# Attention and two gated layers on one core: a pair's reciprocals made one step earlier and sent ahead of the half's bulk loads, and the raw keys' load moved behind them

## The chip, the cores and the metric

The kernel runs on 1 core of one Trainium2 chip. The metric is the device time of one execution in microseconds (us). Before the change the median of 3 runs is 1176.01 us (1171.54 to 1176.41).

## The reference, cut to what matters

```python
def _attn_ref(q, k, v):                      # 4 x 8 heads, 1152 positions, 64 wide
    q_pool = q.reshape(B, H, S // 2, 2, D).mean(axis=3)
    scores = scale * np.matmul(q_pool, k.transpose(0, 1, 3, 2))
    scores = scores - np.max(scores, axis=-1, keepdims=True)
    attn = np.exp(scores)
    attn = attn / (np.sum(attn, axis=-1, keepdims=True) + 1e-09)
    return np.matmul(attn, v)

x = attn_out.transpose(0, 2, 1, 3).reshape(2304, 512)
h = x @ moe_w_in;  x = (h - np.tanh(h)) @ moe_w_out                 # 512 -> 2048 -> 512
h = x @ moe2_w_in; x = (h / (1.0 + np.exp(-1.702 * h))) @ moe2_w_out
```

Each attention row is divided by its sum of exponentials at the end. The change touches only when the reciprocals of these sums are made and sent, and when the keys of a later pair are loaded.

## The kernel before, in words

Two heads make a pair, and there are 16 pairs. The 576 pooled queries of a pair are worked on in two halves of 288, so there are 32 halves: half h belongs to pair h // 2, and an even half is a pair's first one. All 32 halves stand in one loop (L668), with one order of instructions per engine and no scheduler: what is written first is issued first. The attention takes about the first 390 us; the two gated layers behind it are not touched.

In a half, the tensor engine (PE) makes nine score tiles `sc` (`scores`, L414: keys and queries are each split into a rounded high part, `kh`, `qh`, and a rest, `kl`, `ql`; the fourth product, `sel` with `row`, subtracts the row maxima), the scalar engine (ACT) exponentiates them to `pf`, and PE multiplies these with the values (`products`, L473, tile `acc`). Between the score tiles PE makes products `mx` for the row maxima of the next pair (`unit`, L344), which the vector engine (DVE) reduces (L371). The PSUM pool has four buffers, taken in turn by `sc`, `mx` and `acc`.

- The maxima go from columns to a row by DMA: `send_rows` (L380) transposes them (`tt`) and issues small DMAs from SP's queue to `row` and `cr`. Six of them are issued late in an odd half (L388); the first score tile of the next even half needs them.
- The sums of a finished pair go the other way: `sums` (L509) sends them into columns at the start of the next pair's even half (tile `s`), `recip` (L519) adds two parts and takes reciprocals on DVE (L522, L523) and writes them to memory (`rd`, L525), `spread` (L528) reads them back spread over 64 partitions (`rbd`, two DMAs, L531) at the start of the odd half, and `normalise` multiplies with them at that half's end.
- The loads: `load_k` (L287) brings the raw keys `kr` of a pair two ahead (576 KB, two buffers), `load_v` (L292) the values of the next pair (576 KB), `load_sum` (L284) the summed queries `qs` of the pair two ahead (288 KB), `fetch_low` (L339) the queries' low parts `ql` (288 KB). SP issues all of these. GpSimd (POOL) issues two adding DMAs a pair (L281, L338).
- In the next odd half ACT rounds the queries and then the raw keys (`prep_qh`, L306; `prep_kh`, L321); POOL makes the low parts of the keys (`prep_kl`, L328), one part at the end of an even half, one at the end of an odd half. On POOL `kl` waits, by a dependence added by hand, for the job that stands in `last["v"]` (L330): in an even half that is the pair's reciprocal.
- On DVE stand also `rest` additions (L464), `end_rows` (L392) and steps that convert weights (`wt`, L143 to L163), one step a half.

Named places in a half set the order: `first` and `start` ahead of the score tiles, `load`, `pre` and `gp` behind them, then `products`, then `end` and `pool`.

Of the kernel before, what the change touches and what calls it, by code (L numbers as in the profile page):

```python
# [23 lines left out]
def f32(ap):  # L24
    return ap.bitcast(F32)
# [3 lines left out]
def tile_pooled_attention_two_moe(  # L29
# [189 lines left out]
    def attention(ctx: ExitStack):  # L219
# [19 lines left out]
        rows = [ap.tile([128, SP], F32R, name=f"row{i}") for i in range(2)]  # L239
# [133 lines left out]
        def max_rows(p, part, out=None):  # L373
            d = pairs[p]
            mt = f32(d["mt"][:, 0:30]).rearrange("p (c j) -> p j c", c=3)
            at, n = (0, 6) if part == 0 else (6, 4)
            out = d["m3"][:, at:at + n] if out is None else out
            nc.vector.tensor_reduce(out, mt[:, at:at + n, :], AX.X, ALU.min)

        def send_rows(p, part):  # L380
            d = pairs[p]
            tt = ap.tile([128, 32], F32R, tag="tt", name="tt", bufs=2)
            nc.vector.transpose(f32(tt[:]), f32(d["m3"][:]))
            for c in range(6 * part, 6 + 4 * part):
                j, s = divmod(c, 2)
                row = f32((d["row"] if j < 4 else d["cr"])[:])
                q0 = 128 * j if j < 4 else 0
                nc.sync.dma_start(  # L388
                    out=row[64 * s:64 * s + 1, q0:q0 + 128].rearrange("o (a i) -> o a i", i=32),
                    in_=f32(tt[c:c + 97:32, :]))  # L390

        def end_rows(p):  # L392
            d = pairs[p]
            nc.vector.tensor_reduce(
                d["row"][:, 512:], f32(d["cr"][:]).rearrange("p (h i) -> p i h", h=2),
                AX.X, ALU.min)
# [17 lines left out]
        def scores(g, some=slice(0, 4)):  # L414
            p, i = divmod(g, 2 * KT)
            x, t = divmod(i, KT)
            d = pairs[p]
            sc = opened.pop(g, None)
            if sc is None:
                sc = ps.tile([128, 2, 512], F32, tag="ps", name="sc")  # L420
            else:
                some = slice(3, 4)
            ks, xs = slice(128 * t, 128 * t + 128), slice(HB * x, HB * x + HB)
            steps = (
                (d["kh"][:, ks], d["qh"]), (d["kl"][:, ks], d["qh"]),
                (d["kh"][:, ks], d["ql"]), (sel, d["row"]))
            for n, (w, m) in list(enumerate(steps))[some]:
                for s, r in enumerate(sides):
                    nc.tensor.matmul(  # L429
                        sc[:, s, 0:HB], w[r], m[r, xs], start=(n == 0), stop=(n == 3))  # L430
            if some.stop < 4:
                opened[g] = sc
                return
            pf = ap.tile([128, 2, HB], F32, tag="pf", name="pf", bufs=10)
            nc.scalar.activation(pf, sc[:, :, 0:HB], AF.Exp, scale=SCALE)  # L435
            probs[g] = pf

        def add(p, x, t):
            new = probs[(2 * p + x) * KT + t]
            if t == 0:  # L440
                parts[p, x] = new
                return
            out = parts[p, x]
            if t == 1:
                out = ap.tile([128, 2, HB], F32, tag="sum", name="sum")
            job = nc.gpsimd.tensor_add(out, parts[p, x], new)  # L446
            parts[p, x] = out
            return job

        def full(p, x):  # L450
            return 1 < 2 * p + x < 2 * NPAIR - 1

        def rest_of(p, x):
            return ((5, 6, 7, 8),) if full(p, x) else ((5, 6), (7, 8))

        def add_rest(p, x, t):
            n, group = next((n, g) for n, g in enumerate(rest_of(p, x)) if t in g)
            new = probs[(2 * p + x) * KT + t]
            if t == group[1]:
                rests[p, x, n] = ap.tile([128, 2, HB], F32, tag=f"two{5 + 2 * n}", name="rest")  # L460
                prev = probs[(2 * p + x) * KT + group[0]]
            else:
                prev = rests[p, x, n]
            job = last["rest"] = nc.vector.tensor_add(rests[p, x, n], prev, new)  # L464
            if full(p, x) and t == group[1]:
                after(add(p, x, KADD - 1), job)

        def add_two(p, x, t):
            two = [probs[(2 * p + x) * KT + i] for i in (t - 1, t)]
            pairs[p]["twos"].append(ap.tile([128, 2, HB], F32, tag=f"two{t}", name="two"))  # L470
            nc.vector.tensor_add(pairs[p]["twos"][-1], *two)
# [74 lines left out]
        def at(h, when, fn, *args):  # L546
            jobs.setdefault((h, when), []).append(lambda: fn(*args))

        def do(h, when):
            for job in jobs.pop((h, when), ()):  # L550
                job()
# [3 lines left out]
        NH = 2 * NPAIR  # L555
# [32 lines left out]
        for p in range(NPAIR):  # L588
            h = 2 * p
            if p > 0:  # L590
                at(h - 2, "load", load_v, p)
                if p == 1:
                    at(h - 2, "pre", prep_corner, p)
                    at(h - 2, "end", prep_ql, p)
                    at(h - 2, "pool", prep_kl, p, 0)
                    at(h - 1, "end", prep_kl, p, 1, nc.vector)
                else:
                    at(h - 2, "pool", prep_kl, p, 0)
                    at(h - 1, "pool", prep_kl, p, 1)
                    at(h - 1, "first", fetch_low, p, "ql")  # L600
                at(h, "start", sums, p - 1)
                at(h, "pre" if h == NH - 2 else "end", recip, p - 1)
                at(h + 1, "start", spread, p - 1)
                at(h + 1, "end", normalise, p - 1)
            if p > 1:
                at(h - 4, "start", new_pair, p)
                at(max(h - 6, 0), "start", load_one, p)
                at(max(h - 6, 0), "gp" if p > 2 else "start", load_other, p)
                at(h - 4, "load", load_sum, p)
                at(h - 4, "first", load_k, p)  # L610
                at(h - 3, "pre", prep_qh, p)
                at(h - 3, "pre", prep_corner, p)
                at(h - 3, "pre", minus_qh, p)
                at(h - 3, "pre", prep_kh, p, 0)
                at(h - 3, "pre", prep_kh, p, 1)
                at(h - 3, "gp", take_qh, p)
# [13 lines left out]
        first, second = slice(0, 128), (slice(128, 2 * 128), slice(2 * 128, 3 * 128))  # L630
# [37 lines left out]
        for h in range(NH):  # L668
            p, x = divmod(h, 2)
            do(h, "first")  # L670
            do(h, "start")
            g = h * KT
            t = 0
            late = [t for g in rest_of(p, x) for t in g[1:]] if h < NH - 1 else []
            for u in todo[h]:
                if u is None:
                    scores(g + t)
                    if h < NH - 1 and t < KADD - full(p, x) or t < 4:
                        add(p, x, t)
                    elif h == NH - 1 and t in (5, 7):  # L680
                        add_two(p, x, t)
                    t += 1
                    if t == KT and late and h != 1:
                        add_rest(p, x, late.pop(0))
                    continue
                unit(*u)
                if u == (p + 1, 6):
                    max_rows(p + 1, 0)
                    send_rows(p + 1, 0)
                if u == (p, 10):  # L690
                    max_rows(p, 1)
                    send_rows(p, 1)
                if t == KT and late:
                    add_rest(p, x, late.pop(0))
                    if late and x == 0 and full(p, x):
                        add_rest(p, x, late.pop(0))
                        end_rows(p)
            while late:
                add_rest(p, x, late.pop(0))
            if h == NH - 2:  # L700
                end_rows(p)
            do(h, "load")
            do(h, "pre")
            do(h, "gp")
            products(p, x)
            if x == 0 and not full(p, x):
                end_rows(p)
            do(h, "end")
            do(h, "pool")
# [603 lines left out]
    with tc.manual_schedule():  # L1313
        with ExitStack() as c1:
            ending = attention(c1)
        with ExitStack() as c2:
            moe(c2, ending)
# [44 lines left out]
```

## Time and profile before

| | |
|---|---|
| median of 3 runs | 1176.01 us (1171.54 to 1176.41) |
| profiled execution, its own time | 1176.05 us |
| its span, first to last instruction | 1174.3 us |
| mean granted clock of TensorE | 0.998 |
| PE busy | 1161.6 us (99%) |
| DVE busy | 992.5 us (85%) |
| ACT busy | 652.9 us (56%) |
| POOL busy | 453.6 us (39%) |

The profiled execution took 1.75 us more than its span. Busy times are those of the whole span; in a chain of work, each step is named by what it waited for or by the instruction before it on its engine.

### The profile page before, as it was taken

How to read it: one execution, taken by the hardware profiler on the slowest of the kernel's cores; microseconds unless marked ns; L12 is line 12 of the kernel's file. 1: busy time of each engine (PE TensorE's matmuls, PEld its weight loads, DVE VectorE, ACT ScalarE, POOL GpSimd, SP SyncE). 2: the span in 40 equal slices, each digit the busy share in tenths (PEclk: the TensorE clock that was granted, in tenths of full speed). 3: DMA queues.
4: the chain of work that ended last, by engine and by line, in shares of the span. 5: the costliest groups of instructions: out<-in, count | busy, mean ns of one | idle time of the engine just before them, and what ended most of it. 6: DMA issues, size and time to landing. Idle time of an engine off the chain costs nothing.

```text
span 1174.3 us, 23203 instructions
## 1 busy us (share of the span) xinstructions
PE 1161.6 (99%) x9260; PEld 971.5 (83%) x9260; DVE 992.5 (85%) x1242; ACT 652.9 (56%) x969; POOL 453.6 (39%) x321
## 2 busy tenths in 40 slices
PE   9999999999999999999999999999999999999998
PEld 7767676767777888888898898898889999999996
DVE  6888988878988799999999999998986899886442
ACT  4667566656665678676666666655654333342220
POOL 7667676766766223333232333221000222222211
PEclk9999999999999999999999999999999999999999
DMA  6455655555542021111111111112998757765512
GB/s 191 123 118 137 162 127 133 146 143 130 125 111 62 12 64 36 55 54 37 54 36 54 37 36 36 37 54 95 389 389 311 275 215 287 269 225 206 206 54 90
DMA packets 58221, 156.29 MB, mean 133 GB/s; under 512 B 14080, under 2 KB 19712, under 8 KB 58112
## 3 DMA queue, kind: packets, MB, share of 16 engines
q1 hardware_dynamic: 53536, 146.14, 35.8%
q0 software_dynamic: 4032, 8.26, 4.9%
q8 instruction: 73, 1.20, 0.4%
q10 hardware_dynamic: 544, 0.39, 0.1%
q14 instruction: 36, 0.29, 0.1%
HBM read 124.39 MB, written 33.69 MB: 135 GB/s over the span
## 4 chain that ended last, share of the span: by engine, by line
PE 77%; DVE 14%; ACT 4%; issue 2%; DMA 1%; POOL 1%; SPq 1%; DVEq 0%; ACTq 0%; POOLq 0%
PE sc L429 13%; PE y L1048 13%; PE y L1236 12%; PE h L1139 11%; PE acc L480 11%; PE b L996 5%; PE a L996 3%; PE c L996 3%; PE mx L359 3%; DVE work L1182 2%; DVE work L1199 2%; DVE wt L149 2%; DVE wt L143 1%; ACT work L1180 1%; PE acc L493 1%
## 5 line engine op out<-in xcount | busy, mean ns | idle before, releaser
L371 DVE TENSOR_REDUCE mt<-mx 128x2 fp32r<-128x1024 f32 (+2 forms) x176 | 198.1, 1136 | 41.0 <-PE mx L359 22.1
L435 ACT ACTIVATE pf<-sc 128x576 f32<-128x576 f32 x288 | 173.8, 655 | 24.2 <-PE sc L429 15.1
L1236 PE MATMUL y<-mem,big 128*128 128x512 f32 (+1 forms) x780 | 185.1, 368 | 1.2 <-POOL mem L1153 1.2
L1236 PEld LDWEIGHTS y<-mem,big 128*128 128x128 f32 x780 | 142.6, 188 | 21.2 <-POOL mem L1153 2.3
L1034 POOL TENSOR_TENSOR mem<-work,mem 128x768 fp32r<-128x768 f32 x24 | 46.2, 1938 | 289.4 <-ACT mem L1029 274.4
L446 POOL TENSOR_TENSOR sum<-sum,pf 128x576 f32<-128x576 f32 x95 | 137.4, 1446 | 29.2 <-DVE rest L464 23.9
L480 PE MATMUL acc<-pf,v 128*32 128x288 f32 x2304 | 146.3, 407 | 0.0
L1139 PE MATMUL h<-mem,big 128*128 128x512 f32 (+1 forms) x564 | 127.1, 377 | 0.0
L480 PEld LDWEIGHTS acc<-pf,v 128*32 128x32 f32 x2304 | 71.6, 110 | 65.6 <-ACT pf L435 5.0
L1139 PEld LDWEIGHTS h<-mem,big 128*128 128x128 f32 x564 | 104.4, 188 | 17.0
L1153 POOL TENSOR_TENSOR mem<-work,mem 128x1024 fp32r<-128x1024 f32 (+1 forms) x40 | 89.1, 2227 | 75.9 <-ACT mem L1151 75.9
L1048 PE MATMUL y<-big,mem 128*128 128x512 f32 x405 | 114.0, 390 | 0.0
L1201 ACT ACTIVATE work<-work 128x1024 f32<-128x1024 f32 (+1 forms) x40 | 39.1, 977 | 107.5 <-DVE work L1199 107.5
L429 PE MATMUL sc<-qh,kh 64*128 64x288 f32 x576 | 94.0, 315 | 0.0
L171 POOL TENSOR_TENSOR big<-wt,big 128x512 fp32r<-128x512 f32 x25 | 32.6, 1302 | 155.5 <-ACT big L170 142.5
L429 PE MATMUL sc<-row,sel 64*128 64x288 f32 x576 | 88.5, 293 | 3.9 <-DMA row<-tt 2.4
L1048 PEld LDWEIGHTS y<-big,mem 128*128 128x128 f32 x405 | 76.0, 188 | 15.5
L429 PE MATMUL sc<-qh,kl 64*128 64x288 f32 x576 | 87.5, 293 | 0.0
L429 PE MATMUL sc<-ql,kh 64*128 64x288 f32 x576 | 87.2, 292 | 0.0
L1139 PE MATMUL h<-mem,w 128*128 128x512 f32 (+1 forms) x376 | 84.7, 377 | 0.0
L501 ACT ACTIVATE u<-acc 128x576 f32<-128x576 f32 x30 | 19.6, 653 | 107.3 <-PE acc L493 107.3
L1139 PEld LDWEIGHTS h<-mem,w 128*128 128x128 f32 x376 | 69.6, 188 | 11.3
(176 smaller groups left out, 2580.5 us busy)
## 6 DMA issues: line engine op xcount, KB each, us to landing
mem<-x SPq DMA_DIRECT2D x36, 768.0 KB
big<-x SPq DMA_DIRECT2D x27, 768.0 KB
raw<-in_moe_w_in_dram SPq DMA_DIRECT2D x32, 512.0 KB
raw<-in_moe_w_out_dram SPq DMA_DIRECT2D x32, 512.0 KB
v<-in_v_dram SPq DMA_DIRECT2D x16, 576.0 KB
x<-big SPq DMA_DIRECT2D x12, 768.0 KB
kr<-in_k_dram SPq DMA_DIRECT2D x15, 576.0 KB
rbd<-rd SPq DMA_DIRECT2D x32, 144.0 KB
```

Of the source, the lines that this page charges most:

```text
L371: nc.vector.tensor_reduce(out, src, AX.X, ALU.max, negate=True)
L429: nc.tensor.matmul(sc[:, s, 0:HB], w[r], m[r, xs], start=(n == 0), stop=(n == 3))
L435: nc.scalar.activation(pf, sc[:, :, 0:HB], AF.Exp, scale=SCALE)
L446: job = nc.gpsimd.tensor_add(out, parts[p, x], new)
L480: nc.tensor.matmul(acc[32 * n:32 * n + 32, 0], pairs[p]["v"][:, s, t, 32 * h:32 * h + 32], new[t][:, s, :], start=(t == 0), stop=(t == KT ...
L996: nc.tensor.matmul(bank[nm][:, fp, 0:G], w[:, wo, a, 128 * c:128 * c + 128], x[:, b, c, :], start=(k == 0), stop=(k == 5))
L1034: eng.tensor_tensor(g[:, :, 1], halves[n][:, fp], f32(g[:, :, 0]), op=ALU.subtract)
L1048: nc.tensor.matmul(y, gts[2 * side + fp][:, j, r, 128 * t:128 * t + 128], wo[:, p, :], start=(k == 0), stop=(k == len(terms) - 1))
L1139: nc.tensor.matmul(hb[:, j, 0:TBS[b]], wi[:, c, w, :], x[r][c], start=(k == 0), stop=(k == 3 * NKC - 1))
L1153: eng.tensor_tensor(gt[:, :, 1, :], g, f32(gt[:, :, 0, :]), op=ALU.subtract)
L1201: nc.scalar.activation(a, u, AF.Relu, bias=-T2)
L1236: nc.tensor.matmul(ys[m][:, 0:w], lhsT, rhs, start=(fp == 0 and not low and j == p == 0), stop=(fp == 1 and low and j == 1))
```

## The change

Three lines change. The reciprocals of pair p - 1 are made at a new place, `rows`, which is run right behind `end_rows` in an even half; before, they were made at the half's `end`, behind `products`. The load of the raw keys of pair p moves from the start of half 2p - 4 (`first`) to its `load` place, where it is the last in the list.

```diff
-                at(h, "pre" if h == NH - 2 else "end", recip, p - 1)
+                at(h, "pre" if h == NH - 2 else "rows", recip, p - 1)
...
                 at(h - 4, "load", load_sum, p)
-                at(h - 4, "first", load_k, p)
+                at(h - 4, "load", load_k, p)
...
                     if late and x == 0 and full(p, x):
                         add_rest(p, x, late.pop(0))
                         end_rows(p)
+                        do(h, "rows")
```

On SP's queue, from the even half of pair 2 to the rows that its odd half sends, the order before was this (`s` the sums, `qd` the queries in memory, `r` the reciprocals):

```order
L290 DMA kr<-in_k_dram 128x1152
L514 DMA s_101<-u 64x1x9 x4
L278 DMA qd<-in_q_dram 128x576
L388 DMA row_96<-tt 1x4x32 x2
L388 DMA cr_98<-tt 1x4x32 x2
L294 DMA v<-in_v_dram 128x1152
L285 DMA qs<-qd 128x576
L525 DMA rd<-r_1310 128x9
L342 DMA ql<-qd 128x576
L531 DMA rbd<-rd 64x576 x2
L388 DMA row_97<-tt 1x4x32 x6
```

And it is this now:

```order
L514 DMA s_101<-u 64x1x9 x4
L278 DMA qd<-in_q_dram 128x576
L388 DMA row_96<-tt 1x4x32 x2
L388 DMA cr_98<-tt 1x4x32 x2
L525 DMA rd<-r_1255 128x9
L294 DMA v<-in_v_dram 128x1152
L285 DMA qs<-qd 128x576
L290 DMA kr<-in_k_dram 128x1152
L342 DMA ql<-qd 128x576
L531 DMA rbd<-rd 64x576 x2
L388 DMA row_97<-tt 1x4x32 x6
```

`rd` has gone ahead of `v` and `qs`, and `kr` from the top to a place between `qs` and `ql`.

SP's DMAs use eight semaphores in turn (DMAHW0 to DMAHW7), and each waits on its own for the DMA that used it before. Now, from `kr` on, these waits are:

```order
L290 DMA kr<-in_k_dram 128x1152 [waits DMAHW2_49,Pool_49]
L342 DMA ql<-qd 128x576 [waits DMAHW3_49,DMASW4_49]
L531 DMA rbd<-rd 64x576 [waits DMAHW7_49,DMAHW4_49]
L531 DMA rbd<-rd 64x576 [waits DMAHW5_49]
L388 DMA row_97<-tt 1x4x32 [waits DMAHW6_49,DVE_49]
L388 DMA row_97<-tt 1x4x32
L388 DMA row_97<-tt 1x4x32 [waits DMAHW0_49]
L388 DMA row_97<-tt 1x4x32 [waits DMAHW1_49]
L388 DMA row_97<-tt 1x4x32 [waits DMAHW2_49]
L388 DMA row_97<-tt 1x4x32 [waits DMAHW3_49]
```

The fifth of the six row DMAs now waits for the landing of `kr` (DMAHW2), the sixth for that of `ql` (DMAHW3); before, these two waited for `rd` and `ql`.

On DVE, at the end of the same even half, this piece of the difference shows the move:

```order
 L464 TENSOR_TENSOR rest<-rest,pf 128x576 x2
 L394 TENSOR_REDUCE row_96<-cr_98 128x64
-L371 TENSOR_REDUCE mt_90<-mx 128x2
-L156 SCALAR_TENSOR_TENSOR wt<-wa,wt 128x512
-L522 TENSOR_REDUCE r_1310<-s_101 128x9
-L523 RECIPROCAL r_1310<-r_1310 128x9
+L522 TENSOR_REDUCE r_1255<-s_101 128x9
+L523 RECIPROCAL r_1255<-r_1255 128x9
+L371 TENSOR_REDUCE mt_90<-mx 128x2
+L156 SCALAR_TENSOR_TENSOR wt<-wa,wt 128x512
 L371 TENSOR_REDUCE mt_90<-mx 128x2 x2
```

The two instructions of the reciprocal now stand ahead of the half's last reduction of maxima and of the weights' step; in every second even half that step is L143 in place of L156.

## Rows read from the trace of the kernel before

**Rows 1.** The chain that ended last: start, length (us), what.

```profile
81.52 4.50 PE acc L480 x72
...
94.73 4.50 PE acc L480 x72
...
106.34 4.50 PE acc L480 x72
...
118.03 4.50 PE acc L480 x72
...
164.50 4.50 PE acc L480 x72
...
188.41 4.50 PE acc L480 x72
...
234.93 4.50 PE acc L480 x72
...
261.77 4.50 PE acc L480 x72
```

**Rows 2.** Stretch, length; busy PE, PEld, DVE, ACT, POOL; clock, DMA share, GB/s.

```profile
254.10:257.60 3.50, 3.50 (x32) 3.50 (x32) 1.90 (x4) 1.74 (x3) 1.02 (x1) 0.51 0.58 171
```

**Rows 3.** SP's queue in time, halves 6 and 7: start, length (us), DMA.

```profile
94.56 0.38 SPq L294 DMA_DIRECT2D v<-in_v_dram  x1
...
100.60 0.33 SPq L525 DMA_DIRECT2D rd<-r  x1
...
104.48 1.92 SPq L531 DMA_DIRECT2D rbd<-rd  x2
106.50 3.28 SPq L388 DMA_DIRECT2D row<-tt  x6
```

**Rows 4.** SP's queue in time, halves 18 and 19.

```profile
240.76 0.33 SPq L525 DMA_DIRECT2D rd<-r  x1
...
246.21 2.15 SPq L531 DMA_DIRECT2D rbd<-rd  x2
248.45 3.29 SPq L388 DMA_DIRECT2D row<-tt  x6
```

**Rows 5.** DVE in time: the transpose ahead of half 19's rows.

```profile
245.45 0.21 DVE L383 STREAM_TRANSPOSE tt<-m 128x32 f32<-128x32 f32 x1
```

**Rows 6.** DMA in two stretches of halves 6 and 18 (columns as in rows 2).

```profile
94.60:99.10 4.50, 4.50 (x78) 2.41 (x80) 4.40 (x6) 0.60 (x2) 2.12 (x3) 1.00 0.62 197
...
240.00:246.20 6.20, 6.20 (x88) 5.88 (x88) 5.07 (x10) 5.78 (x10) 5.96 (x6) 1.00 0.74 153
```

**Rows 7.** ACT in time, half 7: the keys' rounding and the next idle time.

```profile
108.14 1.24 ACT L321 ACTIVATE kh<-kr 128x576 fp32r<-128x576 f32 x2
111.40 0.66 ACT L501 ACTIVATE u<-acc 128x576 f32<-128x576 f32 x1 [2.02 <-PE acc L493]
```

**Rows 8.** DVE in time, the end of half 8.

```profile
121.76 0.28 DVE L394 TENSOR_REDUCE row<-cr 128x64 fp32r<-128x128 f32 x1
121.96 1.21 DVE L371 TENSOR_REDUCE mt<-mx 128x2 fp32r<-128x1024 f32 x1
123.09 0.68 DVE L156 SCALAR_TENSOR_TENSOR wt<-wa,wt 128x512 f32<-128x512 f32 x1
...
123.90 0.21 DVE L523 RECIPROCAL r<-r 128x9 f32<-128x9 f32 x1
124.03 1.22 DVE L371 TENSOR_REDUCE mt<-mx 128x2 fp32r<-128x1024 f32 x1
```

**Rows 9.** POOL in time: `kl` of half 8, and two sums of half 18.

```profile
124.20 1.43 POOL L328 TENSOR_TENSOR kl<-kr,kh 128x576 fp32r<-128x576 f32 x1 [3.07 <-DVE r L523]
...
232.10 2.93 POOL L446 TENSOR_TENSOR sum<-sum,pf 128x576 f32<-128x576 f32 x2
```

**Rows 10.** DVE in time: the same addition beside an idle and a busy POOL.

```profile
81.95 0.75 DVE L464 TENSOR_TENSOR rest<-pf 128x576 f32<-128x576 f32 x1
...
234.29 1.36 DVE L464 TENSOR_TENSOR rest<-pf 128x576 f32<-128x576 f32 x1
```

## The prediction

> **What bounds the kernel now.** I read the shares of busy time first, then the chain of work that ended last through the attention, and then the timelines of SP and DVE where that chain was interrupted. PE is busy 99% of the span, so only what PE loses can be won. The chain is a row of `acc` steps, and from one to the next a half can be timed: half 6 to 7 takes 106.34 - 94.73 = 11.61 us, half 7 to 8 takes 118.03 - 106.34 = 11.69, the two together 23.30 [rows 1]. Three stretches are longer: half 5 to 6 takes 94.73 - 81.52 = 13.21, that is 1.52 over; halves 12 to 14 take 23.91, 0.61 over; halves 18 to 20 take 26.84, 3.54 over [rows 1]. Together 5.67 us. In the third, PE ran 3.50 us at a granted clock of 0.51, about the lower of its levels (1.2 of 2.4 GHz), after it had stood still; so a good half of that loss is clock and not waiting [rows 2].
>
> What is late there is the row of maxima. In half 19 the transpose `tt` is done at 245.45 + 0.21 = 245.66 [rows 5], but SP issues the six row DMAs only from 248.45 to 251.74, right behind `rbd`, which waited until 246.21 for `rd`, issued at 240.76 [rows 4]. In half 7 it is the same queue with less delay: `rd` 100.60, `rbd` 104.48, rows from 106.50 to 109.78 [rows 3]. Counted from the odd half's `acc`, the rows of half 7 are out 109.78 - 106.34 = 3.44 us into it and cost nothing; those of half 19, whose `acc` would stand at 234.93 + 11.61 = 246.54, are out after 5.20 us and cost 3.54 [rows 1, 3, 4]. The limit lies between.
>
> **The change part by part.** No instruction is added or removed; all the cost is in order and waiting.
>
> *The reciprocal and `rd` earlier.* At the end of half 8 DVE runs the last reduction of maxima, the weights' step and the two instructions of the reciprocal from 121.96 to 124.03, and the reciprocal ends at 123.90 + 0.21 = 124.11 [rows 8]. In the new order the reciprocal comes first. Its two instructions take about twice 0.21, so it ends at about 122.38, 1.73 us earlier. In half 18 `rd` would then go at about 239.1 to 239.3 in place of 240.76. Its landing took up to 246.21 - 240.76 = 5.45 us before, 3.88 in half 6 [rows 3, 4], with `v` and `qs` ahead of it; now these are behind it. `rbd` takes 2.15 us to issue and must begin by 243.6 to be out of the way of `tt`; that leaves `rd` over 4.2 us. I take it that this is enough. Then the rows start when `tt` is ready, at about 245.8, and are out at 249.1, 2.6 us into the half in place of 5.20; half 7's 3.44 was harmless. All three losses go: -5.67 us. Its bounds are 0 and 5.67.
>
> *The price: the bulk loads later, and `kr` among them.* SP issues in order, so `v`, `qs` and `kr` now stand behind a wait for the reciprocal. In half 6, `v` went at 94.56 [rows 3]; it will go at about 99.4. `v` is wanted a half later, which covers this. The keys are closer: from 94.60 to 99.10 the DMA engines moved 197 GB/s, 887 KB in 4.50 us, which is `v` and `qs` (864 KB); beside an adding DMA of POOL it was 153 GB/s in half 18 [rows 6]. `v`, `qs` and `kr` are 1440 KB, so 7.3 to 9.4 us, and `kr` is there at 106.7 to 108.8. ACT wants it at 108.14, and after rounding it is idle 2.02 us before its next work [rows 7]. A wait of up to 0.7 is hidden there: nothing. Without that cover it would be 14 times 0.7.
>
> *`ql` and the lanes of the row DMAs.* `ql` makes it 1728 KB, 8.8 to 11.3 us from 239.6 in half 18: it lands at 248.4 to 250.9. The sixth row DMA now waits for it through its semaphore, and would be issued at 245.8 + 2.75 = 248.5 otherwise. At the better rate that costs nothing; at the worse one the rows are out at 251.4, 4.9 us into the half, nearly as late as before. I take the better: 197 GB/s is an average with a start and a tail in it, and the share of the DMA engines was only 0.62. This is the weakest step.
>
> *`kl` earlier on POOL.* `kl` waits for the reciprocal by hand; in half 8 POOL had been idle 3.07 us before it started at 124.20, 0.09 after the reciprocal's end [rows 8, 9]. Now it runs from about 122.47 to 123.90, and the weights' step, which starts 0.34 later than its 123.09, at 123.43, meets it. What such a meeting does is seen in half 18: the addition `rest` took 1.36 us in place of 0.75 and ended 0.62 after POOL's sums did (235.65 and 235.03) [rows 9, 10]. So the step should end at 124.5 in place of 124.1, and the reduction behind it starts 0.4 later than 124.03. PE fills that reduction's buffer again soon after; how much of the 0.4 it feels no row shows, between 0 and 0.4. I take 0.3. It applies to the halves with this step and no other work on POOL, 4, 8, ... 28: 7 times 0.3 is +2.1 us, with bounds 0 and 2.8.
>
> The Trainium skill has a rule for this, in "SBUF — State Buffer", section "Who interferes with whom": a DVE instruction with two SBUF inputs and a GpSimd one that reads SBUF share one port pair, and whoever comes second is blocked until the first has finished. By that rule the block is real, and the whole wait of 0.47 us counts, 7 times 0.47 is 3.3 us at most, where the row gives 2.8; it also says that the reciprocal and the reductions, with one input, are not held. The trace agrees with its first part by the 1.36 us.
>
> *The last reduction of an even half later.* It ends 0.42 us later, at 121.96 + 1.21 + 0.42 = 123.59 in half 8 [rows 8]. Its buffer goes to the second score tile of the next half, which PE makes right behind the product that DVE begins to reduce at 124.03. So it should just be in time: 0, at worst 14 times 0.42, 5.9 us.
>
> *`kr` no longer at the top of the even half.* The sums, `qd` and the rows' second part go out sooner. No PE wait of the three losses hangs on them: 0.
>
> **Sum.** The profiled execution took 1176.05 us, the median of the runs is 1176.01, so no correction is needed. 1176.05 - 5.67 + 2.1 = 1172.5 us. The lowest run of before, 1171.54, is 4.5 below the others, about as much as the losses above: they do not come in every execution, so the change may win less against such a run.
>
> **The rivals.**
> - *The stalls go and the port costs nothing* (PE has slack at the reduction): 1176.05 - 5.67 = 1170.4. For it: `acc` follows `acc` in 11.6 to 11.7 us whatever DVE does. Against: DVE's reduction started with no idle time before it [rows 8].
> - *The rows stay late* because `ql` or `kr`, now in front of them, lands late: in the three bad halves nothing is won and the port is still paid, 1176.05 + 2.1 = 1178.2. For it: 153 GB/s in half 18 [rows 6].
> - *Slower: the burst makes every pair's rows late.* The place is the sixth row DMA's wait for `ql`. It decides once `ql` lands more than about 2 us behind 248.5 in the measure of half 19. A loss like that of half 5 in each of 14 odd halves: 14 times 1.52 is 21.3, 1176.05 - 5.67 + 2.1 + 21.3 = 1193.8. Against: only half 18 shows a slow adding DMA beside the loads at that rate.
> - *Nothing of it reaches PE* (the rows are late for another reason and POOL's port costs nothing): 1176.
>
> **How the numbers follow.** Forecast 0.40, no port cost 0.20, rows stay late 0.20, slower 0.10, nothing 0.10. The likeliest gives 1172.5, with a range of its own of 1170.4 to 1174.5. The range takes in the second, third and fifth case as well: 1169.8 to 1179.5. A change of 0.5%, 5.9 us, is about what a measurement of this kernel can tell from none: faster means under 1170.1, slower over 1181.9. Of the no-port case half would fall under 1170.1 (0.10), and a little of the forecast (0.05): faster 0.15; slower 0.10, the fourth case; same 0.75.
>
> **What would show it.** Right: `rbd` no longer waits for `rd` up to the rows, the row DMAs begin within 0.2 us of `tt`, no PE wait for `row` in halves 6, 14 and 20, no stretch at half clock in the attention; in halves 4, 8, ... 28 a weights' step of about 1.1 us beside `kl`, and a half longer by 0.3. Wrong: SP waits for `kr` or `ql` between two row DMAs; ACT idle ahead of `kh` for over 2 us; PE waiting for DVE at the second score tile of each odd half; or all of this as said and the time unchanged.

## The result: slower by 0.7%

| | before | after |
|---|---|---|
| median of 6 runs each | 1174.78 us (1171.54 to 1176.41) | 1182.62 us (1180.90 to 1184.51) |
| profiled execution, its own time | 1176.05 us | 1180.9 us |
| its span | 1174.3 us | 1179.1 us |

The ratio is 1.0071, with a 95% interval of 1.0052 to 1.0089. The forecast was 1172.5 us with a range up to 1179.5: the time lies outside it, on the slow side.

The chain that ended last, through the attention (start, length, what), tells where the time went:

```profile
46.65 4.50 PE acc L480 x72
...
82.07 4.50 PE acc L480 x72
...
99.20 2.33 DVE wt L143
...
106.92 4.50 PE acc L480 x72
...
130.41 4.50 PE acc L480 x72
...
381.68 4.50 PE acc L480 x72
```

The same chain before, at halves 2 and 30:

```profile
46.76 4.50 PE acc L480 x72
...
376.64 4.50 PE acc L480 x72
```

From half 2 to half 30 the chain now takes 381.68 - 46.65 = 335.03 us; before it was 376.64 - 46.76 = 329.88, so the attention holds all of the loss: 5.15, beside 4.8 between the spans. The pair of halves 5 and 6 takes 106.92 - 82.07 = 24.85 us, where before halves 6 and 7 together took 23.30 [rows 1]. Halves 7 and 8 take 130.41 - 106.92 = 23.49. New in the chain is a weights' step on DVE, L143, with 2.33 us.

What PE waited for from 40 to 350 us (total, times, longest):

```profile
PE mx L359 <- DVE mt L371: 6.8, 6, 1.3
PE sc L429 <- DMA row<-tt: 0.5, 1, 0.5
```

The same view of before has no wait of PE for DVE, but this one, and 1.2 us more for which no releaser is named:

```profile
PE sc L429 <- DMA row<-tt: 2.4, 3, 1.6
```

PE's weight loads, listed in a view of their own, waited 14.8 us for DVE's reductions, and 4.8 before. So the old losses are gone and a longer wait for DVE's reductions has taken their place. DVE at the end of halves 6, 8 and 26 (start, length, instruction):

```profile
98.03 1.17 DVE L371 TENSOR_REDUCE mt<-mx 128x2 fp32r<-128x1024 f32 x1
99.11 2.42 DVE L143 TENSOR_SCALAR wt<-raw 128x512 int32<-128x512 int32 x1
101.44 1.21 DVE L371 TENSOR_REDUCE mt<-mx 128x2 fp32r<-128x1024 f32 x1
...
122.33 0.28 DVE L394 TENSOR_REDUCE row<-cr 128x64 fp32r<-128x128 f32 x1
...
122.74 0.22 DVE L523 RECIPROCAL r<-r 128x9 f32<-128x9 f32 x1
...
123.95 1.05 DVE L156 SCALAR_TENSOR_TENSOR wt<-wa,wt 128x512 f32<-128x512 f32 x1
...
340.76 1.55 DVE L143 TENSOR_SCALAR wt<-raw 128x512 int32<-128x512 int32 x1
```

POOL in the same three places:

```profile
98.93 0.85 POOL L281 DMA_DIRECT2D qd<-in_q_dram  x1
99.51 1.72 POOL L328 TENSOR_TENSOR kl<-kr,kh 128x576 fp32r<-128x576 f32 x1
...
123.04 1.41 POOL L328 TENSOR_TENSOR kl<-kr,kh 128x576 fp32r<-128x576 f32 x1 [1.33 <-DVE r L523]
...
340.60 1.44 POOL L328 TENSOR_TENSOR kl<-kr,kh 128x576 fp32r<-128x576 f32 x1
```

Each weights' step that meets `kl` ends about 0.3 to 0.6 us after `kl` does: 101.53 after 101.23, 125.00 after 124.45, 342.31 after 342.04. For L156 the step grew from 0.68 [rows 8] to 1.05, as forecast. For L143 it grew far more, and PE sat idle behind it:

```profile
102.71 0.50 PE L359 MATMUL mx<-kh,qh 64*128 64x512 f32 x2 [1.29 <-DVE mt L371]
```

By DVE's groups from 40 to 350 us the seven L143 took 14.4 us and the six L156 6.3, against 3.1 and 4.1 before. SP's queue, on the other hand, did what it was meant to do; halves 6 and 7 [rows 3]:

```profile
98.14 0.33 SPq L525 DMA_DIRECT2D rd<-r  x1
...
106.09 3.28 SPq L388 DMA_DIRECT2D row<-tt  x6
```

SP's waits from 40 to 350 us:

```profile
SPq L388 <- DVE tt L383: 35.9, 13, 4.3
...
SPq L531 <- DMA rd<-r: 5.6, 7, 1.0
...
SPq L388 <- DMA ql<-qd: 1.1, 5, 0.4
SPq L388 <- DMA kr<-in_k_dram: 1.1, 2, 0.8
```

And of before:

```profile
SPq L531 <- DMA rd<-r: 31.8, 13, 4.6
```

`rbd` waited 31.8 us for `rd` before and 5.6 now, and the rows start when `tt` is ready. They are out at 109.37, 109.37 - 106.92 = 2.45 us into half 7, where it was 3.44.

### The profile page after: what moved, and what is told of

The parts are those of the page before. It is cut to its first block, busy times and chain, and to the rows that moved or that the text cites. A ratio compares the mean times of both kernels' runs of the same rounds, so it can differ in the third digit from the quotient of the medians.

```text
span 1179.1 us, 23215 instructions
## 1 busy us (share of the span) xinstructions
PE 1162.6 (99%) x9260; PEld 970.3 (82%) x9260; DVE 1005.4 (85%) x1242; ACT 652.6 (55%) x969; POOL 453.6 (38%) x321
## 4 chain that ended last, share of the span: by engine, by line
PE 67%; DVE 23%; ACT 5%; issue 4%; POOL 1%; DMA 0%; DVEq 0%; SPq 0%; ACTq 0%; POOLq 0%
PE y L1049 12%; PE y L1237 11%; PE sc L429 10%; PE h L1140 10%; PE acc L480 7%; PE b L997 5%; DVE mt L371 3%; PE a L997 3%; PE c L997 3%; DVE wt L143 3%; PE mx L359 2%; DVE rest L464 2%; DVE work L1200 2%; DVE work L1183 2%; DVE wt L156 2%
## 5 line engine op out<-in xcount | busy, mean ns | idle before, releaser
L429 PE MATMUL sc<-row,sel 64*128 64x288 f32 x576 | 85.7, 292 | 0.8 <-DMA row<-tt 0.5
L1140 PEld LDWEIGHTS h<-mem,w 128*128 128x128 f32 x376 | 69.6, 188 | 11.3
```

The lines of the kernel that those rows point to most:

```text
L429: nc.tensor.matmul(sc[:, s, 0:HB], w[r], m[r, xs], start=(n == 0), stop=(n == 3))
L1140: nc.tensor.matmul(hb[:, j, 0:TBS[b]], wi[:, c, w, :], x[r][c], start=(k == 0), stop=(k == 3 * NKC - 1))
```

## The experiments

Two theories stood at the start. **Port:** `kl`, released earlier, blocks DVE's weights' step, and that is all the loss. **Burst:** the bulk loads, three in a row and late, hold the rows or the keys. Each diff is against the changed kernel unless said otherwise.

**1. `kl` waits for the weights' step,** L143 and L156 (`last["v"]` is the job for which POOL's `kl` waits):

```diff
-            nc.vector.tensor_scalar(
+            last["v"] = nc.vector.tensor_scalar(
...
-            nc.vector.scalar_tensor_tensor(
+            last["v"] = nc.vector.scalar_tensor_tensor(
```

> The changed kernel, with POOL's kl of an even half made to wait for that half's weights' step (L143 or L156) in place of the reciprocal, as it did in effect before the change. Theory (POOL's kl, released early by the early reciprocal, runs into DVE's weights' step and holds it up): the even halves fall back to 11.5 to 11.6 us, L143 to about 0.45 us from 2.42, L156 to 0.69 from 1.05, the three old losses stay away, and the time is 1168 to 1172. If the issue of POOL's adding DMA alone also holds L143 up, its halves keep 0.3 to 0.5 us each and the time is 1171 to 1174. Rival (the burst of loads behind the reciprocal, or the later last reduction, is what costs): the time stays at 1180 to 1184 and the even halves at 11.8 and 13.1.

Measured: 1183.80 us (1181.12 to 1188.27, 6 runs), ratio to before 1.0076 (1.0051 to 1.0101). That is a miss: the time is that of the rival, though the even halves are as the theory had them. The block was gone (the seven L143 took 2.9 us, the six L156 4.1), and yet the time was no better. The profiled run is the slowest of the six. Its chain:

```profile
95.62 4.50 PE acc L480 x72
107.25 4.50 PE acc L480 x72
122.56 4.50 PE acc L480 x72
134.05 4.50 PE acc L480 x72
```

Half 6 takes 11.63 us and half 8 takes 11.49, so even halves are as short as they get; but half 7 takes 15.31. SP's waits from 40 to 350 us:

```profile
SPq L388 <- DMA kr<-in_k_dram: 9.7, 8, 1.6
...
SPq L388 <- DMA ql<-qd: 4.2, 10, 1.5
```

SP's queue in halves 6 and 7:

```profile
100.02 0.33 SPq L525 DMA_DIRECT2D rd<-r  x1
...
101.86 0.38 SPq L342 DMA_DIRECT2D ql<-qd  x1
...
106.40 4.83 SPq L388 DMA_DIRECT2D row<-tt  x6
```

PE's waits, same stretch:

```profile
PE sc L429 <- DMA row<-tt: 7.4, 8, 1.7
PE sc L429 <- issue: 4.5, 3, 1.7
```

The six row DMAs take 4.83 us in place of 3.28, because the last ones wait for `kr` and `ql` on the semaphores that they share. In half 7 it is the sixth, which waits 1.5 us for `ql`. They are out at 111.23, 3.98 us into the half. Then PE stands 1.74 us ahead of the product that reads `row` (one of the waits under `issue`, for which the view names no releaser), and part of the loss is clock again: from 116 to 122 us the granted clock was 0.78, a mean between its two levels (stretch, length; busy PE, PEld, DVE, ACT, POOL; clock, DMA share, GB/s):

```profile
116.00:122.00 6.00, 6.00 (x69) 5.66 (x66) 3.70 (x7) 4.38 (x8) 4.28 (x3) 0.78 0.19 50
```

In six of the odd halves the chain itself goes from the issue of `ql` to its landing and on through the sixth row DMA. For the rows of half 11:

```profile
151.97 9.06 DMA ql<-qd
...
161.04 3.19 DMA row<-tt
```

ACT's rounding of the keys waited too, 5.1 us for `kr` in 7 waits, but up to half 30 no piece of the chain is on ACT. So the burst is real, and in the changed kernel something kept it from showing.

**2. The keys' move alone** (against the kernel before):

```diff
-                at(h - 4, "first", load_k, p)
+                at(h - 4, "load", load_k, p)
```

> The kernel before with the second part of the change alone: raw keys' load at the load place, reciprocal at the end as before. Theory (port): kl still waits for the late reciprocal, so no half is longer through DVE; rd now stands behind v, qs and kr, so rbd and the rows are later in more odd halves than before: 1176 to 1184, with PE waits for row. Rival (the burst of loads costs by itself, whatever the reciprocal does): over 1180 with DVE's steps longer or ACT waiting for keys. If neither: 1172 to 1177.

Measured: 1172.75 us (1169.71 to 1174.70, 10 runs), ratio 0.9985 (0.9969 to 1.0001): as good as nothing. The expected rise, with late rows in more odd halves, did not come; the third case did. With the reciprocal late, `v`, `qs` and `kr` leave before `rd`, and early. In the profiled run, the slowest of the ten, half 7 still took 120.50 - 105.16 = 15.34 us by the chain.

**3. The reciprocal's move alone, with experiment 1's guard:**

```diff
-                at(h - 4, "load", load_k, p)
+                at(h - 4, "first", load_k, p)
```

> The first part of the change alone (reciprocal early, rd ahead of v and qs), raw keys' load where it was before, and kl of an even half waiting for the weights' step. Theory: the early rd alone takes the three losses away, so 1168 to 1172, like the version with the keys moved too. Rival (it is the keys' load out of the rows' way that took the losses away): the losses stay in part, 1173 to 1177.

Measured: 1170.13 us (1169.60 to 1171.04, 12 runs), ratio 0.9969 (0.9957 to 0.9982). No stall is left. Its chain takes 371.75 - 47.64 = 324.11 us from half 2 to half 30:

```profile
47.64 4.50 PE acc L480 x72
...
82.43 4.50 PE acc L480 x72
...
105.74 4.50 PE acc L480 x72
...
128.91 4.50 PE acc L480 x72
...
371.75 4.50 PE acc L480 x72
```

**4. `kl` freed in the kernel before** (against the kernel before; `kl` then waits for an older job):

```diff
-            last["v"] = nc.vector.reciprocal(r9, r9)
+            nc.vector.reciprocal(r9, r9)
```

> The kernel before, with kl of an even half no longer waiting for the reciprocal (it waits for an older job of DVE); nothing else is moved. Theory: kl starts right behind POOL's adding DMA; in halves 4, 8, ... 28 it is done before L156 begins and costs nothing; in halves 6, 10, ... 26 it stands behind the weights' split and the adding DMA while L143 comes due, and if POOL's queue goes first, L143 takes over 1.5 us and those halves 0.7 to 1.5 us more: 1178 to 1184. If L143 slips in behind the split: 1172 to 1177. Rival (burst of loads): 1172 to 1177 and no half changed.

Measured: 1184.71 us (1184.17 to 1187.39, 4 runs), ratio 1.0095 (1.0068 to 1.0122). The size is about that of the block, but the expected place, L143, is a miss: L143 and L156 kept their 0.45 and 0.68 us. `kl` ran so early that it met the additions `rest`: in half 8 two of them took 3.34 us in place of 1.98, and PE's weight loads waited for them:

```profile
PEld acc L493 <- DVE rest L464: 6.1, 7, 1.2
```

It shows that a `kl` let go too early costs PE something wherever it lands, but it doesn't isolate the weights' step.

**5. The reciprocal's move alone, no guard:**

```diff
-                at(h - 4, "load", load_k, p)
+                at(h - 4, "first", load_k, p)
```

> The first part of the change alone, as written (reciprocal and rd early, kl waits for the reciprocal), raw keys' load where it was before. Theory of two costs that hide each other (kl against the weights' step on DVE; the burst of v, qs and kr ahead of the rows): only the first cost is here, read from the changed kernel's trace as about 1.5 us in halves 6 to 22, 0.7 in half 26, 0.3 in halves 2, 4, 8, ... 28, in all 10.9, and the three old losses (5.7) are away: 1178 to 1182. Rival (without the keys in the burst the steps do not meet, since rd and kl come at other times): 1169 to 1173.

Measured: 1181.46 us (1180.79 to 1181.83, 4 runs), ratio 1.0061 (1.0039 to 1.0083), as expected: the seven L143 took 14.4 us again and the six L156 6.3. The guard is all that parts it from experiment 3. The block alone costs as much as block and burst together:

| median, us | `kl` free | `kl` behind the weights' step |
|---|---|---|
| keys in the burst | 1182.62 (the change) | 1183.80 |
| keys at `first` | 1181.46 | 1170.13 |

Either cost brings the time from 1170 to between 1181 and 1184; the second adds nearly nothing. Not all were measured beside the same runs: the kernel before had a median of 1174.78 beside the change, 1174.03 beside the column's 1183.80 and 1170.13, and 1173.50 beside 1181.46.

**6. The keys ahead of `rd`, with the guard:** `load_k` goes to a new place behind `send_rows(p, 1)`.

```diff
-                at(h - 4, "load", load_k, p)
+                at(h - 4, "keys", load_k, p)
...
                     send_rows(p, 1)
+                    do(h, "keys")
```

> Both parts and kl waiting for the weights' step, but the raw keys' load goes right behind the row DMAs of the even half, ahead of rd, so it does not wait for the reciprocal. Theory (the burst behind rd is the second cost): the burst is v and qs alone again, no row DMA waits for kr, 1168 to 1172, at or a little under the version with the keys at the half's start. Rival (the keys' load anywhere in the second part of the even half costs): PE waits for row as with all three in the burst, 1178 to 1186.

Measured: 1170.32 us (1169.94 to 1170.80, 9 runs), ratio 0.9971 (0.9958 to 0.9983). So the keys' load does no harm late in the even half, as long as it goes ahead of `rd`.

**7. The values out of the burst, the keys left in it, with the guard:**

```diff
-                at(h - 2, "load", load_v, p)
+                at(h - 2, "load" if p == 1 else "first", load_v, p)
```

> Both parts and kl waiting for the weights' step; the raw keys stay last in the burst behind rd, but the values' load (576 KB) goes to the start of the even half in its place. Theory (it is the amount behind rd, 1440 KB, that makes the row DMAs wait): 864 KB are left, kr and ql land ahead of the fifth and sixth row DMA, 1168 to 1173. Rival (it is kr's own place, since the fifth row DMA waits for it): these waits stay, 1178 to 1186.

Measured: 1169.77 us (1169.58 to 1170.42, 8 runs), ratio 0.9960 (0.9944 to 0.9976). This is the best version. The order of `kr`, `ql` and the rows is that of the change here, and so are the semaphores that the rows share, but there are 576 KB less in front:

```profile
98.67 0.39 SPq L342 DMA_DIRECT2D ql<-qd  x1
...
103.73 3.29 SPq L388 DMA_DIRECT2D row<-tt  x6
```

The rows need 3.29 us again. So it is the amount in the burst, and not the shared semaphore as such, that makes them late.

**8. Only L156 meets `kl`:** the guard stands at L143 alone, and the keys go at `first`.

```diff
-            nc.vector.tensor_scalar(
+            last["v"] = nc.vector.tensor_scalar(
```

> The reciprocal early, raw keys at the half's start as before, kl of an even half waiting for L143 but not for L156: in halves 4, 8, ... 28 kl still meets the weights' step. Theory: L156 takes 1.05 us in these seven halves and they are 0.3 longer (11.8 in place of 11.48), the others are 11.6: 1171 to 1174, about 2.1 over the version without any meeting. Rival: no difference to it.

Measured: 1172.65 us (one run). The six L156 took 6.3 us, the seven L143 2.9. The run is 2.5 us above experiment 3, but that is one run, beside other runs of the kernel before. Its chain says the same:

```profile
46.84 4.50 PE acc L480 x72
...
373.24 4.50 PE acc L480 x72
```

From half 2 to half 30 it takes 326.40 us, 2.29 more than in experiment 3.

**9. The adding DMA behind `kl`,** with the keys at `first` and no guard:

```diff
-                at(max(h - 6, 0), "gp" if p > 2 else "start", load_other, p)
+                at(max(h - 6, 0), "late" if p > 2 else "start", load_other, p)
...
             do(h, "pool")
+            do(h, "late")
```

> As recip_alone (reciprocal early, raw keys at the half's start, kl waits for the reciprocal), but POOL issues the pair's first adding DMA (L281) behind kl and not ahead of it. Theory (L143 is held up by whatever POOL runs when it comes due, the adding DMA's issue and then kl): with the issue gone from in front, kl starts sooner and L143 takes about 1.55 us in halves 6 to 22, as it did in half 26, where there is no such issue, in place of 2.4; those halves come down from 13.1 to about 12.3: 1176 to 1179. Rival (kl alone holds it, wherever the issue stands): L143 stays at 2.4 and the halves at 13.1, 1180 to 1182.

Measured: 1176.14 us (one run; the kernel before 1175.13 beside it), 5.3 below the median of experiment 5, which was measured beside other runs. The seven L143 took 10.1 us in place of 14.4. The order on POOL is turned round:

```profile
98.36 1.44 POOL L328 TENSOR_TENSOR kl<-kr,kh 128x576 fp32r<-128x576 f32 x1
99.73 0.84 POOL L281 DMA_DIRECT2D qd<-in_q_dram  x1
```

and on DVE the step is held by `kl` alone:

```profile
98.52 1.56 DVE L143 TENSOR_SCALAR wt<-raw 128x512 int32<-128x512 int32 x1
```

## Why the prediction was wrong, point by point

**The step that failed** is "`kl` earlier on POOL", in its last sentences: "It applies to the halves with this step and no other work on POOL, 4, 8, ... 28: 7 times 0.3 is +2.1 us". The mechanism was right, and the forecast place came as said; but the halves 2, 6, 10, ... 26 were left out, with a cost of nothing. There the weights' step is L143, and in five of them POOL also issues an adding DMA just ahead of `kl`. Those halves hold most of the price. The chain shows it against experiment 3:

- Halves 5 and 6 with L143 and the adding DMA: 24.85 us against 105.74 - 82.43 = 23.31 (its half 5 starts at 82.43), 1.54 longer. Five such pairs: 7.7.
- Halves 7 and 8 with L156: 23.49 against 128.91 - 105.74 = 23.17, 0.32 longer. Seven such pairs: 2.2, the predicted 2.1.
- Half 26, where L143 meets `kl` without an adding DMA: 0.7. Half 2, where the issue ended 1.3 us before `kl` began and L143 took 0.80: 0.3.

The sum is 10.9, and the two chains differ by 335.03 - 324.11 = 10.92. The old losses that went were worth 329.88 - 324.11 = 5.77, so the net is +5.15. With +10.9 in place of +2.1, the prediction's own sum would have given 1176.05 - 5.67 + 10.9 = 1181.3; the profiled execution took 1180.9. It is the fastest of the six; the median is 1.7 above it, and no trace shows what the other five lost. The order of DVE under the change names L143 as the step of every second even half, so the omission could be seen there. The kernel before could not show the block: `kl` waited for the reciprocal, and that stood behind the weights' step on DVE, so the two never met. The change moved the reciprocal ahead of that step and so took a guard away that nobody had written down.

The section of the Trainium skill that the prediction named, "SBUF — State Buffer", "Who interferes with whom", also says that a `tensor_scalar`, with its one input, can contend with GpSimd, when it runs in a two-port mode. The prediction used only the two-input rule. L143 is a `tensor_scalar`; no row names its mode, but the trace agrees that it is held, by the 1.55 us of half 26, which end 0.27 after `kl`. The 2.42 us, begun 0.40 before `kl` by the profile, are taken up in the last section.

**The step called the weakest** would have failed too. It took `ql` to land in time, at the better DMA rate. In experiment 1 SP did wait for `kr` and `ql` between the row DMAs. In half 7 `ql` let the sixth go at about 106.40 + 5 x 0.55 + 1.5 = 110.65, 10.2 us after the first of the loads (100.45): between the two bounds (8.8 and 11.3), and too late. The prediction also named `ql` alone, where the fifth row DMA's wait for `kr` was the larger part, 9.7 us against 4.2. That is the rival "slower: the burst makes every pair's rows late", with its place right. Its 1193.8 was too much: the median was 1183.8, and in the profiled run, the slowest, nine odd halves from 3 to 25 were longer than in experiment 3, by 0.7 to 3.6 us.

**Why the two costs don't add up.** The block holds PE in the even half, behind `rd` and the burst, and so the odd half begins later against the burst. In the changed kernel `rd` went 106.92 - 98.14 = 8.78 us before half 7's `acc`; in experiment 1 only 107.25 - 100.02 = 7.23. The rows were out 2.45 and 3.98 us into the half. The rows of before, 3.44, cost nothing, and those of its half 5, out at 82.00 + 3.28 - 81.52 = 3.76, cost 1.52, so the limit lies between the two. That the lead over the burst is the reason was read from these traces and fits the table of four; no run set the lead by itself. And it can't be the whole reason: behind the halves with L156 the lead differs by only 0.3 us (half 17: 227.09 - 219.66 = 7.43, and 230.16 - 223.05 = 7.11 in experiment 1), yet there the six rows were out 9.89 us after `rd` in the changed kernel and 11.14 in experiment 1. In that half the loads themselves came later; why stays open.

**What held.** All three old losses went, worth 5.77 by the chain (5.67 predicted). The reciprocal was to end 1.73 us earlier: in half 8 it ends 122.96 - 122.33 = 0.63 us after the start of `end_rows`, where before it was 124.11 - 121.76 = 2.35 [rows 8], 1.72 earlier. `rd` landed in time, and the rows start with `tt`: in half 19 this had been put at 2.6 us into the half, and half 7 now shows 2.45. The later last reduction costs nothing by itself: experiment 3 has the same order on DVE and no stall. The keys' rounding on ACT waited once for `kr` from 40 to 350 us, 0.3 us. Two workings were slightly off, and nothing turned on them: the share of clock in the loss of halves 18 to 20 is 3.50 x 0.49 = 1.7 of 3.54 us, a little under half; and 1440 and 1728 KB, in units of 1024 bytes, were divided by GB/s of 1000, so the times for the loads are 2.4% too short. The remark that the losses do not come in every execution held as well: the kernel before spread from 1170.62 to 1178.35 in 23 runs, experiment 3 beside it from 1169.60 to 1171.04, so the gain against a median run is 3.9, not 5.7.

## What to carry to other kernels

Before an instruction is moved, look for what waits for it by hand, and ask what it had been kept from meeting; a dependence can guard a stretch that its code does not name. Cost a block like this in every variant of the place (here L143 and L156, with and without an adding DMA), for the variant left out held four fifths of the price. And when taking away a shown cause changes nothing, look for a second cost under it before dropping the theory: a table of four, with each cost in and out, showed this.

## What the hardware showed unexpectedly

- A DVE step with one input was held as fully as one with two: L143 took 0.42 us alone, 1.56 beside `kl`, and 2.42 beside `kl` with an adding DMA's issue ahead of it. The reductions showed nothing of the kind: one of 1.22 us ran beside `kl` in experiment 3, and others, beside no `kl`, took as long. Who begins first seems to matter: in half 26 of experiment 4 L143 began 0.13 us before `kl` and took only 0.45, while `kl` took 1.62. The next point has a case that doesn't fit this.
- The issue of the adding DMA does not hold L143 by itself. In experiment 3 L143 started 0.17 us into it and took 0.42, since `kl` was not released yet:

```profile
99.27 0.85 POOL L281 DMA_DIRECT2D qd<-in_q_dram  x1
99.99 1.58 POOL L328 TENSOR_TENSOR kl<-kr,kh 128x576 fp32r<-128x576 f32 x1
```

  DVE beside it:

```profile
99.44 0.42 DVE L143 TENSOR_SCALAR wt<-raw 128x512 int32<-128x512 int32 x1
```

  In the changed kernel L143 also started 0.18 us into the issue, with `kl` released, and was held from then on, though the profile puts `kl` 0.40 us later. All five halves with that issue ahead show this, 2.39 to 2.42 us. Whether a released `kl` takes hold while POOL still issues, or the profile's start of `kl` is late (spans on POOL are rough), stays open. The expectation of experiment 9 put it down to the issue itself; this row speaks against that.
